# A Fourier filter and a gated feed-forward block in one kernel: the first transform step on sums and differences of rows, in 32x32 tiles

## Chip, cores, metric

The kernel runs on one core of one Trainium2 chip. The metric is the device time of one launch in microseconds (us). Its engines are named as in the profile: PE (TensorE, matmuls; PEld its weight loads), DVE (VectorE), ACT (ScalarE), POOL (GpSimd) and SP (SyncE, which only issues DMAs). ACT and POOL issue DMAs too.

## The reference

```python
batch, seq, dim = (8, 3008, 256)              # d_ff = 1536

def _attn_ref(x, filt_r, filt_i):
    X = np.fft.rfft(x, axis=1)
    F = (filt_r + 1j * filt_i)[None, :, :]
    return np.fft.irfft(X * F, n=x.shape[1], axis=1)

def _moe_ref(x, w_gate, w_val, w_out):        # x: (8 * 3008, 256)
    g = x @ w_gate
    silu = g * (1.0 / (1.0 + np.exp(-g)))
    return silu * (x @ w_val) @ w_out
```

All is float32. The first function filters each of the 8 batches along its 3008 tokens; the second is applied to every token of the result.

## The kernel before

**Two kinds of work in one stream.** The feed-forward block of batch b and the Fourier filter of batch b + 1 run side by side. A batch has 12 steps (`Group`: four chunks of tokens by three groups of hidden columns). Each step follows one written order of 174 tokens, `SCHEDULE`: a token names one small piece of work, and every engine gets its instructions in the order of the tokens (`pin` keeps the program's order). The tokens that the text needs:

- `Q0`, `P1`, `Q2` ...: matmuls of two 188-column halves into a PSUM bank k0 to k3 (L1075, tiles wk); `A13`, `A01`, `B..`, `E..` likewise into banks a.. and e.. (wa, we). `W1`, `W2`, `W6`: matmuls of the output projection (L1172, tiles wA, wF, wG).
- `f1`: ACT writes k1 negated into SBUF (L1090). `c1`, `c0`: ACT copies k1 and k0 (L1094). `g1`, `g0`: ACT's silu (L1117).
- `x03`, `s13`, `s01`: DVE combines a bank k with f1 or with a difference D (`D01`, by POOL); `s13` and `s01` write it into the banks a13 and a01 (L1097), to which `A13` and `A01` then add. `y01`: DVE combines k1 with c0 (L335). `h0`, `h1`: DVE's product with g0, g1 (L1122).
- `o1`, `o2`: the projection's sums, by DVE or, for the first of three groups, ACT (L328, L1184). `z0.o`: a DVE transpose, after the third group only. `x0.o` and so on: output stores.
- `b0` to `b7`: one part each of a burst of the next batch's filter. They stand at places 5, 10, 11, 33, 37, 95, 104 and 117 of the 174.

The order around the change, in one step:

```
Q0 o3' z1.o' t4.2' W2 b0 f0 S00' S01' i0 b1 b2 x0.o' t0.0 x1.o' i1 Q1 t0.1 x2.o' P3 x3.o' f1 t4.3'
W1 x4.o' S10' x03 S11' D01 i2 i3 i4 s13 b3 x5.o' P1 o1 b4 t0.2 P0 o2 z0.o c1 i5 A13 g1 c0 S20' Q2
S21' g0 y01 m13 t1.0 h0 f2 s01 W6 t1.1 h1 x23 D02 P2 o6 D12 A01 ...
```

PSUM has seven banks in turn for these tiles (pool `wps`, `NB`). After use of a part of `wt_t`, SP loads the next step's weights into it (`reload_weights`, L493), and waits for the matmuls that still read it.

**The filter's bursts.** From batch 2 on, the transform goes in two kinds of bursts, run during the batch before: `quads(g)`, g = 0 to 3, in steps 0 to 3, and `fours(w)`, w = 0 to 6, in steps 4 to 10. `load` is a DMA on SP (L618).

`quads` does the transform over 47 rows. A piece u holds four columns of rows n and the same four 32 further; rows lie on partitions 0 to 46 and 64 to 110. At `b0` there are eight matmuls (L716, tiles wqa, 47 rows in, 64 columns out, 512 elements). At `b1` and `b2` ACT copies one bank of a piece and DVE forms the difference and the sum with the other bank. At `b3` and `b4` ACT issues the stores of the two pieces to DRAM (`d1`, L733) and SP the loads of the next ones (`load_x`). `load_x(0)` and `load_x(1)` come in step 11 of the batch before.

`fours` loads these rows again (`load_four`), does a second transform step, and multiplies with the filter. For the complex product it swaps rows of a copy by DMA (`lent<-raw`), and multiplies by an imaginary part of the filter whose sign alternates by row. The rows with the other sign were negated once: during batch 1, `negated_filter` loads them to SBUF, ACT negates them (L323), and they are stored to `f_dram`; `keep_filter` copies the others in DRAM.

**Places in memory.** `room_of(tag)` gives parts of one SBUF tile, `lent`: `x` (two rooms), `y`, `g`, `e`, `t`, `tb`, `f`. `quads` uses x, y and g; `fours` uses the others too.

Of the kernel before, what the change touches and what calls it, by code (L numbers as in the profile page):

```python
# [41 lines left out]
FP32 = mybir.dt.float32  # L42
# [57 lines left out]
S00 S01 W1 S20 S21 S10 S11 W5 o1 W2 o5 S30 S31 W6 o2 z0.o o6 W3 o3 z1.o x0.o x1.o x2.o x3.o x4.o  # L100
x5.o W7 q4 o7 z3.o W4 o4 z2.o X0.o X1.o X2.o X3.o X4.o X5.o
""".split()
FILTER_AT = ("f1", "P0", "Q2", "h0", "g3", "A12", "Q0", "P1", "c1", "h1")
BLOCKS = (0, 1, 3, 2)
PAIRS = ((0, 1), (1, 2), (2, 3), (0, 2), (1, 3), (0, 3))
PAIRS_USED = ((1, 3), (0, 1), (0, 2), (1, 2), (2, 3), (0, 3))
# [19 lines left out]
def dft_tables():  # L126
# [40 lines left out]
    quad = np.zeros((128, 64))  # L167
    for h, turn in enumerate((ph, ph + 2 * np.pi * s / (2 * N1))):
        cols = np.stack([np.cos(turn), -np.sin(turn)], 2).reshape(N1, 2 * NS)
        quad[64 * h:64 * h + N1, 0:2 * NS] = cols  # L170

    four = np.zeros((128, N_FOUR + 1, 2, 4, 64))
    lo, qq = np.arange(32), np.arange(32)
# [32 lines left out]
def kernel(  # L206
# [60 lines left out]
    def weights_of(b, k, g):  # L267
        return wt_1 if b == 0 and k < NT and g == 1 else wt_t

    dram_tiles = [wdpool.tile([2 * NS, N2, C], FP32, name=f"d{1 + i % 2}_{i // 2}")  # L270
                  for i in range(4)]
    yt_dram = [wdpool.tile([128, 3 * len(PAIRS), TQ], FP32, name=f"yt_{k}") for k in range(NT)]
    y_dram = [wdpool.tile([128, 8, TQ], FP32, name=f"y_{k}") for k in range(NCHUNK)]
    o_dram = [wdpool.tile([128, 4 * NH, RP], FP32, name=f"o_{k}") for k in range(NT)]
# [32 lines left out]

    def keep_filter(n):

        part, r, e, half = (0, 0, 1)[n // 4], (0, 1, 1)[n // 4], n // 2 % 2, n % 2  # L310
# [4 lines left out]
    def negated_filter(w, stage):  # L315

        t = room_of("et"[w % 2])[0:64].rearrange("p (s c) -> p s c", c=C)
        if stage == 0:
            for q in range(4):
                pin(nc.sync.dma_start(out=t[16 * q:16 * q + 16],  # L320
                                      in_=filter_rows(1, q // 2, q % 2, 4 * w, 4)))
        elif stage == 1:
            pin(nc.scalar.mul(t, t, -1.0))  # L323
        else:
            pin(nc.sync.dma_start(out=f_pairs[:, 0, 1, 4 * w:4 * w + 4], in_=t))

    def add(eng, dst, a, b):
        return eng.tensor_tensor(out=dst, in0=a, in1=b, op=ALU.add)  # L328
# [246 lines left out]
    def load_back():  # L575

        t = rpool.tile([128, 2, 128], U32, name="quad", tag="pw", bufs=3)
        t = t.bitcast(FP32).rearrange("p b f -> p (b f)")
        quad_t.append(t)
        pin(nc.sync.dma_start(out=t[:, 0:64], in_=quad_dram.ap()))  # L580
# [19 lines left out]
    class Spectral:  # L600


        def __init__(self, b):
            self.b = b
            self.d1, self.d2 = [dram_tiles[2 * (b % 2) + i] for i in range(2)]
# [93 lines left out]
        def bank(self, name):  # L699
# [2 lines left out]
                return bank(name).rearrange("p (i c) -> p i c", i=NV)  # L702
            return fbank(name)

        def quads(self, g):

            pieces = (2 * g, 2 * g + 1)
            banks = {}
            for u in pieces:
                xt = self.x.pop(u)  # L710
                for h in range(2):
                    banks[u, h] = bank(f"qa_{self.b}_{u}_{h}")
                for cp in range(2):
                    for h in range(2):
                        r = slice(64 * h, 64 * h + N1)
                        pin(nc.tensor.matmul(  # L716
                            out=banks[u, h][64 * cp:64 * cp + 64], lhsT=quad_t[0][r, 0:64],
                            rhs=xt[r, 2 * cp:2 * cp + 2].rearrange("p n c -> p (n c)"),
                            start=True, stop=True))
            yield  # L720
            t1 = {u: room_of("yg"[i]).rearrange("p (n h c) -> p n h c", h=2, c=C)
                  for i, u in enumerate(pieces)}
            for u in pieces:
                low, high = [banks[u, h].rearrange("p (n c) -> p n c", c=C) for h in range(2)]
                pin(nc.scalar.copy(out=t1[u][:, :, 0], in_=low))
                pin(sub(nc.vector, t1[u][:, :, 1], t1[u][:, :, 0], high))
                pin(add(nc.vector, t1[u][:, :, 0], t1[u][:, :, 0], high))
                yield
            d1 = self.d1.rearrange("a (n h) c -> a n h c", h=2)
            for u in pieces:  # L730
                for cp in range(2):
                    n = 4 * u + 2 * cp
                    pin(nc.scalar.dma_start(out=d1[:, n:n + 2], in_=t1[u][64 * cp:64 * cp + 2 * NS]))  # L733
                self.load_x(u + 2)
                yield
            if g == 3:
                self.load_filter(0)
                self.load_turns(0)
            yield
            if g == 3:  # L740
                self.load_four(0)

        def load_four(self, w):

            if w < N_FOUR:
                t = self.t2[w] = room_of("t").rearrange("p (s h c) -> p s h c", h=2, c=C)
                d1 = self.d1.rearrange("(s r) (n h) c -> s (r n) (h c)", r=2, h=2)
                for p in range(2):
                    s = 4 * w + 2 * p
                    self.load(out=t[64 * p:64 * p + 64].rearrange("p s h c -> p s (h c)"),  # L750
                              in_=d1[s:s + 2].rearrange("s q c -> q s c"))

        def load_filter(self, w):

# [10 lines left out]
        def fours(self, w):  # L765
# [615 lines left out]
    for b in range(B):  # L1381
# [36 lines left out]
        for step in range(NCHUNK * NG + (b == B - 1)):  # L1418
# [16 lines left out]
            for place, token in enumerate(SCHEDULE):  # L1435
# [31 lines left out]
                    continue  # L1467
                if b == 0 and (step, op) == (5, "A23"):
                    nxt.load_two(0)
                if b + 2 < B and (step, op) in ((11, "Q2"), (11, "B01")):  # L1470
                    following.load_x(int(op == "B01"))
                if b == 1 and step < 4 and op in FILTER_AT:
                    n = FILTER_AT.index(op)
                    if n < 4 and step < 3:
                        keep_filter(4 * step + n)
                    elif 4 <= n < 6 and step < 3:
                        negated_filter(2 * step + n % 2, 0)
                    elif n >= 6 and step:
                        negated_filter(2 * step - 2 + n % 2, n // 2 - 2)
# [43 lines left out]
```

## Time and profile before

| | |
|---|---|
| median of 3 runs | 2825.41 us (2821.07 to 2829.73) |
| profiled execution | 2823.7 us; its span in the trace 2821.6 us; granted PE clock 0.997 |
| busy | PE 2787.5, PEld 2319.9, DVE 1999.1, ACT 1564.7, POOL 1579.9 us |
| DMA | 586.59 MB, mean 208 GB/s; the SP queue's packets took 60.8% of 16 engines' span, ACT's 5.7% |
| `quads` matmuls, L716 | 384 records of 589 ns (median), two for each of 192 instructions |
| `quads` copies and sums | ACT 48 of 586 ns; DVE 48 of 684 and 48 of 687 ns |
| `quads` stores, L733 | 96 issues on ACT, 308 to 2747 ns, median 435 |
| negation, L323 | 6 on ACT, 1057 ns each |

A group line of the profile reads: line, engine, operation, what is written and read with shapes, count, busy time and mean, then the idle time of that engine before it with what ended it. A timeline line reads: start in us from the span's start, length, engine, line, operation, tiles and shapes, count, and in brackets the idle time before it with what ended it. `ACTq` and `SPq` are the instruction queues of ACT and SP, which issue DMAs. Times of single steps count from the span's start.

### The profile page before, as it was taken

The page shows a single profiled execution, that of the slowest core. Times are in us where ns is not written, and L with a number is a line of the kernel's source. Part 1 is how long each engine was busy: PE and PEld are TensorE (multiplying, and loading weights), DVE is VectorE, ACT ScalarE, POOL GpSimd, SP SyncE. Part 2 cuts the span into 40 slices and gives each one's busy share as a digit, 9 for nine tenths or more (in the row PEclk, how much of TensorE's full clock was granted, in tenths as well). Part 3 has the DMA queues.
Part 4 walks back from the last instruction along what each step waited for, and adds up shares of the span by engine and source line. Part 5 has one row for each costly group of instructions (what it writes and reads, how often), then busy time and mean ns, then how long its engine had stood idle before and what let it go on. Part 6 is the DMA issues. An engine that isn't in the chain of part 4 may idle for free.

```text
span 2821.6 us, 48540 instructions
## 1 busy us (share of the span) xinstructions
PE 2787.5 (99%) x15444; PEld 2319.9 (82%) x15444; DVE 1999.1 (71%) x4579; ACT 1564.7 (55%) x4176; POOL 1579.9 (56%) x1689
## 2 busy tenths in 40 slices
PE   8999999999999999999999999999999999999998
PEld 6877888888888888788888888878888888888887
DVE  7898767767667766667766677667676767666666
ACT  5675455555555555555555555555555555555554
POOL 4786576465545565456653566445655455545544
PEclk9999999999999999999999999999999999999999
DMA  9687876877666775667666676667766677654443
GB/s 214 224 272 237 283 242 211 285 233 232 181 188 207 246 221 175 204 215 229 222 185 197 211 246 201 188 190 236 228 205 181 213 224 227 192 153 148 153 137 82
DMA packets 362933, 586.59 MB, mean 208 GB/s; under 512 B 198620, under 2 KB 245660, under 8 KB 362536
## 3 DMA queue, kind: packets, MB, share of 16 engines
q1 hardware_dynamic: 337722, 533.61, 60.8%
q10 hardware_dynamic: 22318, 44.38, 5.7%
q0 software_dynamic: 2640, 5.51, 0.7%
q8 instruction: 125, 2.05, 0.3%
q14 instruction: 128, 1.05, 0.1%
HBM read 467.48 MB, written 101.34 MB: 202 GB/s over the span
## 4 chain that ended last, share of the span: by engine, by line
PE 91%; POOL 2%; DVE 2%; DMA 1%; issue 1%; ACT 1%; ACTq 0%; SPq 0%; POOLq 0%; DVEq 0%
PE wa L1075 25%; PE wk L1075 17%; PE wA L1172 16%; PE we L1075 13%; PE wG L1172 8%; PE wF L1172 4%; PE pd L978 3%; PE wqa L716 2%; PE wqc L775 1%; PE wqb L787 1%; POOL out_dram L1157 0%; POOL h L331 0%; PE pa L857 0%; DMA lent<-later_tbl 0%; PE pd L981 0%
## 5 line engine op out<-in xcount | busy, mean ns | idle before, releaser
L1075 PE MATMUL wa<-y_t,wt_t 128*128 128x188 f32 x4464 | 881.6, 324 | 4.0 <-DVE wa L1097 2.3
L1075 PEld LDWEIGHTS wa<-y_t,wt_t 128*128 128x128 f32 x4464 | 749.8, 191 | 79.5 <-ACT wa L1101 9.3
L1075 PEld LDWEIGHTS wk<-y,wt_t 128*128 128x128 f32 x2976 | 495.0, 190 | 109.5 <-issue 33.4
L1075 PE MATMUL wk<-y,wt_t 128*128 128x188 f32 x2976 | 572.0, 325 | 3.2 <-ACT f L1090 3.2
L331 POOL TENSOR_TENSOR h<-h 128x376 f32<-128x376 f32 x572 | 559.6, 1000 | 15.4 <-DVE h L328 15.2
L328 POOL TENSOR_TENSOR h<-h 128x376 f32<-128x376 f32 x190 | 182.8, 983 | 685.5 <-DVE h L1122 685.5
L1172 PE MATMUL wA<-h,wo_t 128*128 128x376 f32 x1532 | 551.8, 482 | 3.9 <-DVE o L328 2.1
L1075 PE MATMUL we<-y_t,wt_t 128*128 128x188 f32 x2232 | 431.7, 323 | 1.6 <-ACT we L1106 1.5
L331 POOL TENSOR_TENSOR D<-f,f 128x376 f32<-128x376 f32 x288 | 280.0, 986 | 258.4 <-ACT f L1090 256.0
L331 DVE TENSOR_TENSOR we<-we,m 128x376 f32<-128x376 f32 x576 | 319.8, 556 | 141.1 <-PE we L1075 73.9
L1075 PEld LDWEIGHTS we<-y_t,wt_t 128*128 128x128 f32 x2232 | 369.3, 190 | 2.7 <-ACT we L1106 2.1
L1172 PEld LDWEIGHTS wA<-h,wo_t 128*128 128x128 f32 x1532 | 274.9, 190 | 113.7 <-issue 7.0
L1110 ACT COPY m<-wa 128x376 f32<-128x376 f32 x576 | 272.7, 473 | 102.0 <-PE wa L1075 98.8
L335 DVE SCALAR_TENSOR_TENSOR y<-wk,c 128x376 f32<-128x376 f32 x480 | 244.8, 541 | 63.8 <-ACT c L1094 37.8
L1117 ACT ACTIVATE g<-wa 128x188 f32<-128x188 f32 x576 | 187.5, 326 | 164.7 <-PE wa L1075 154.9
L1117 ACT ACTIVATE u<-we 128x188 f32<-128x188 f32 x576 | 188.7, 328 | 160.2 <-DVE we L331 153.3
L1172 PE MATMUL wG<-h,wo_t 128*128 128x376 f32 x768 | 274.0, 479 | 0.0
L1094 ACT COPY c<-wk 128x376 f32<-128x376 f32 x288 | 136.5, 474 | 226.0 <-PE wk L1075 196.7
L1090 ACT ACTIVATE f<-wk 128x376 f32<-128x376 f32 x288 | 140.4, 488 | 168.6 <-PE wk L1075 118.0
L1106 ACT COPY we<-y 128x376 f32<-128x376 f32 x480 | 222.3, 480 | 19.8 <-DVE h L1122 14.4
L1122 DVE TENSOR_TENSOR h<-wa,g 128x188 f32<-128x188 f32 x576 | 199.4, 347 | 38.0 <-ACT g L1117 37.6
L1122 DVE TENSOR_TENSOR h<-we,u 128x188 f32<-128x188 f32 x576 | 198.5, 345 | 28.8 <-ACT u L1117 17.3
(193 smaller groups left out, 3523.0 us busy)
## 6 DMA issues: line engine op xcount, KB each, us to landing
wt_t<-w_all SPq DMA_DIRECT2D x174, 896.0 KB
wt_t<-w_all SPq DMA_DIRECT2D x174, 768.0 KB
lent<-filter SPq DMA_DIRECT2D x36, 1024.0 KB
lent<-d SPq DMA_DIRECT2D x84, 256.0 KB
d<-lent ACTq DMA_DIRECT2D x84, 256.0 KB
d<-lent ACTq DMA_DIRECT2D x96, 192.0 KB
lent<-raw SPq DMA_DIRECT2D x144, 128.0 KB
t<-d SPq DMA_DIRECT2D x114, 128.0 KB
```

What stands on the lines that cost most here:

```text
L328: return eng.tensor_tensor(out=dst, in0=a, in1=b, op=ALU.add)
L331: return eng.tensor_tensor(out=dst, in0=a, in1=b, op=ALU.subtract)
L335: return nc.vector.scalar_tensor_tensor(out=dst, in0=a, scalar=-1.0, in1=b, op0=ALU.mult, op1=ALU.subtract)
L978: pin(nc.tensor.matmul(out=rows, lhsT=self.t4[k, i][:, j, ts(cb, 128)], rhs=cols, start=j == 0, stop=True, skip_group_check=True))
L1075: pin(nc.tensor.matmul(out=ps[:, z], lhsT=self.wt[:, SLOT[p], z], rhs=rhs, start=start and z == 0, stop=True, skip_group_check=True))
L1090: pin(act.mul(self.small(f"f{i}", f"f{i}", 1), t[f"k{i}"], -1.0))
L1094: pin(act.copy(out=self.small(f"c{i}", f"c{i}", 1), in_=t[f"k{i}"]))
L1106: pin(act.copy(out=self.bank(f"e{at}"), in_=t[f"y{at}"]))
L1110: pin(act.copy(out=self.small(f"m{at}", "m", 4), in_=t[f"a{at}"]))
L1117: pin(act.activation(out=self.small(op, "g", 3, 1)[:, 0], in_=ps[:, 1], func=AF.Silu))
L1122: pin(v.tensor_tensor(out=dst, in0=ps[:, 0], in1=g, op=ALU.mult))
L1172: pin(nc.tensor.matmul(out=self.tiles[at], lhsT=wo_t[:, JB * q + i, WO[p], :], rhs=self.hs[i][:, HID[p]], start=start and i == 0, stop=Tru ...
```

## The change

From batch 2 on, `quads` works on sums and differences of rows. Row n and row 47 - n of the transform have the same cosine and opposite sines; so 24 sums and 24 differences take the place of 47 rows. The falling rows must first lie in rising order: `turn_rows` copies them in DRAM, row by row, into `turned_dram`. `load_x(g)` loads 32 rising rows for 16 columns (four DMAs, 128 partitions in all) and the turned rows in one DMA of 512 KB. `fold(g)` makes the sums in room `e` and the differences in room `t`, four DVE instructions of 128x512. Those of group g + 1 stand at `b4` to `b7` of the burst before; those of group 0 in step 11 (`first_fold`).

A burst has 16 matmuls of 24 rows in and 32 columns out. The order of what follows changes as well: at `b1` the copy and both sums of the first piece, at `b2` the copy of the second piece and the stores of the first, at `b3` the sums of the second, at `b4` its stores. The rows go to `quads_dram` in a new order, 64 partitions a store for 48; `load_four` reads them with four DMAs for two.

The sign of the swapped rows is now put on by ACT as it copies them (`mul` with a column of +1 and -1 for `copy`). `negated_filter` is gone, and `keep_filter` copies all 16 parts.

```diff
-FILTER_AT = ("f1", "P0", "Q2", "h0", "g3", "A12", "Q0", "P1", "c1", "h1")
+FILTER_AT = ("f1", "P0", "Q2", "h0")
...
-                if u < N_QUAD:
-                    self.x[u] = room_of("x", u).rearrange("p (n c) -> p n c", c=C)
+                if u < N_QUAD // 2:
+                    self.x[u] = [room_of("x", n) for n in range(2)]
+                    up, down = self.x[u]
+                    at = self.turned.rearrange("(g q) p c -> g p q c", q=4)[u]
+                    self.load(out=down.rearrange("p (q c) -> p q c", c=C), in_=at)
                     rows = x[self.b].rearrange("(r n) c -> r n c", n=N2)
-                    for h in range(2):
-                        for a, e in ((0, 32), (32, N1)):
-                            self.load(out=self.x[u][64 * h + a:64 * h + e],
-                                      in_=rows[a:e, 32 * h + 4 * u:32 * h + 4 * u + 4])
+                    for n in range(4):
+                        first = 16 * n + 4 * u
+                        self.load(out=up[ts(n, 32)].rearrange("p (q c) -> p q c", c=C),
+                                  in_=rows[0:32, first:first + 4])
...
+        def turn_rows(self, *parts):
+            xb, to = x[self.b], self.turned
+            end = NS if self.b > 3 else 32
+            for part in parts:
+                h, lane, n = part // 2, 32 * part, 16 * part
+                p = 1 - h
+                self.load(out=to[:, lane + p:lane + end],
+                          in_=bass.AP(tensor=xb.tensor, ap=[[C, 16], [-N2 * C, end - p], [1, C]],
+                                      offset=xb.offset + ((N1 - 1) * N2 + n) * C))
+                if h == 0:
+                    self.load(out=to[:, lane], in_=xb[n:n + 16])
+
+        def fold(self, g):
+            if g < N_QUAD // 2:
+                up, down = self.x.pop(g)
+                self.x[g] = [room_of("e"), room_of("t")]
+                for t, f in zip(self.x[g], (add, sub)):
+                    for half in range(2):
+                        a = ts(half, NV * C)
+                        pin(f(nc.vector, t[:, a], up[:, a], down[:, a]))
+                        if t is self.x[g][1] and half:
+                            self.load_x(g + 1)
+                        yield
+
+        def first_fold(self):
+            for _ in range(4):
+                yield
+            yield from self.fold(0)
...
         def quads(self, g):
...
+            for cp in range(2):
+                for t in range(2):
+                    for i, u in enumerate(pieces):
+                        for h in range(2):
+                            r, c = 32 * (2 * h + i), 32 * (2 * cp + t)
+                            pin(nc.tensor.matmul(
+                                out=banks[u, h][c:c + 32], lhsT=quad_t[0][r:r + NS, ts(t, 32)],
+                                rhs=parts[t][r:r + NS, ts(cp, NV * C)],
+                                start=True, stop=True))
             yield
...
+            low(pieces[0])
+            both(pieces[0])
+            yield
+            low(pieces[1])
+            store(pieces[0])
+            yield
+            both(pieces[1])
+            yield
+            store(pieces[1])
+            next(fold, None)
+            yield
...
-                pin(nc.scalar.copy(out=t, in_=there[p]))
+                pin(nc.scalar.mul(t, there[p], quad_t[0][:, 64:65]))
...
+    for part, at in enumerate(((3, "E23"), (4, "A13"), (4, "E23"), (5, "A13"))):
+        chore(*at, lambda part: following.turn_rows(part), part)
...
+        if b + 2 < B:
+            bursts[-1] = following.first_fold()
...
-                if b + 2 < B and (step, op) in ((11, "Q2"), (11, "B01")):
-                    following.load_x(int(op == "B01"))
+                if b and b + 2 < B and (step, op) == (8, "Q0"):
+                    following.turn_rows(0, 1, 2, 3)
+                if b + 2 < B and (step, op) == (11, "Q0"):
+                    following.load_x(0)
```

`low(u)` is the ACT copy of a piece's first bank, `both(u)` the two DVE instructions, `store(u)` the two store DMAs on ACT. The table for the matmuls is rewritten to 24 rows of cosines and of sines, and gets the column of signs.

More of the change, by code (lines that the diff above doesn't have):

```diff
@@ L165, in dft_tables @@
                 back[row:row + rows, first + N1 * i:first + N1 * (i + 1)] = one_hi[a:a + rows]
[L167 to L170, printed above, removed]
+    quad = np.zeros((4, 32, 2, 32))
+    for h in range(2):
+        turn = 2 * np.pi * (np.outer(2 * n1[0:NS] + h, s) % (2 * N1)) / (2 * N1)
+        quad[2 * h:2 * h + 2, 0:NS, 0, 0:NS], quad[2 * h:2 * h + 2, 0:NS, 1, 0:NS] = np.cos(turn), -np.sin(turn)
+        quad[2 * h:2 * h + 2, 23 * h] *= np.array([0.5, 0.0])[:, None]
+    quad = np.concatenate([quad.reshape(128, 64), np.tile([[1.0], [-1.0]], (64, 1))], 1)
     four = np.zeros((128, N_FOUR + 1, 2, 4, 64))
@@ L271 @@
                   for i in range(4)]
+    quads_dram = [wdpool.tile([64, N2, C], FP32, name=f"quads_{i}") for i in range(2)]
+    turned_dram = [wdpool.tile([16, 128, C], FP32, name=f"turned_{i}") for i in range(2)]
     yt_dram = [wdpool.tile([128, 3 * len(PAIRS), TQ], FP32, name=f"yt_{k}") for k in range(NT)]
@@ L308, in keep_filter @@
     def keep_filter(n):
-        part, r, e, half = (0, 0, 1)[n // 4], (0, 1, 1)[n // 4], n // 2 % 2, n % 2
+        part, r, e, half = n // 8, n // 4 % 2, n // 2 % 2, n % 2
         q = 32 * e + 16 * half
@@ L313, in keep_filter @@
                               in_=filter_rows(part, e, half, 0, NS)))
[L315 to L325, printed above, removed]
     def add(eng, dst, a, b):
@@ L579, in load_back @@
         quad_t.append(t)
-        pin(nc.sync.dma_start(out=t[:, 0:64], in_=quad_dram.ap()))
+        pin(nc.sync.dma_start(out=t[:, 0:65], in_=quad_dram.ap()))
         t = rpool.tile([128, 2, 128, 2], U32, name="back", tag="raw", bufs=2)
@@ L604, in __init__ @@
             self.b = b
+            self.quads_dram, self.turned = quads_dram[b % 2], turned_dram[b % 2]
             self.d1, self.d2 = [dram_tiles[2 * (b % 2) + i] for i in range(2)]
@@ L703, in bank @@
             return fbank(name)
-        def quads(self, g):
[L707 to L719, printed above, removed]
+        def turn_rows(self, *parts):
[9 more added lines that the diff above has]
+                    self.load(out=to[:, lane], in_=xb[n:n + 16])
@@ new lines, in first_fold @@
+        def first_fold(self):
+            for _ in range(4):
+                yield
+            yield from self.fold(0)
+        def quads(self, g):
+            pieces = (g, g + N_QUAD // 2)
+            banks = {(u, h): bank(f"qa_{self.b}_{u}_{h}") for u in pieces for h in range(2)}
+            parts = self.x.pop(g)
+            for cp in range(2):
+                for t in range(2):
+                    for i, u in enumerate(pieces):
+                        for h in range(2):
+                            r, c = 32 * (2 * h + i), 32 * (2 * cp + t)
[3 more added lines that the diff above has]
+                                start=True, stop=True))
@@ L720, in quads @@
             yield
+            fold = self.fold(g + 1)
             t1 = {u: room_of("yg"[i]).rearrange("p (n h c) -> p n h c", h=2, c=C)
                   for i, u in enumerate(pieces)}
[L723 to L728, printed above, removed]
@@ L729, in quads, with low, both @@
-            d1 = self.d1.rearrange("a (n h) c -> a n h c", h=2)
-            for u in pieces:
+            views = {key: t.rearrange("p (n c) -> p n c", c=C) for key, t in banks.items()}
+            def low(u):
+                pin(nc.scalar.copy(out=t1[u][:, :, 0], in_=views[u, 0]))
+            def both(u):
+                pin(sub(nc.vector, t1[u][:, :, 1], t1[u][:, :, 0], views[u, 1]))
+                pin(add(nc.vector, t1[u][:, :, 0], t1[u][:, :, 0], views[u, 1]))
+            d1 = self.quads_dram.rearrange("a (n h) c -> a n (h c)", h=2)
@@ L731, in quads, with store @@
+            def store(u):
                 for cp in range(2):
                     n = 4 * u + 2 * cp
-                    pin(nc.scalar.dma_start(out=d1[:, n:n + 2], in_=t1[u][64 * cp:64 * cp + 2 * NS]))
-                self.load_x(u + 2)
-                yield
+                    pin(nc.scalar.dma_start(out=d1[:, n:n + 2], in_=t1[u][64 * cp:64 * cp + 64]))
+            low(pieces[0])
[4 more added lines that the diff above has]
+            yield
@@ L738, in quads @@
                 self.load_turns(0)
+            next(fold, None)
             yield
@@ L741, in quads @@
                 self.load_four(0)
+            next(fold, None)
+            yield
+            next(fold, None)
         def load_four(self, w):
@@ L746, in load_four @@
                 t = self.t2[w] = room_of("t").rearrange("p (s h c) -> p s h c", h=2, c=C)
-                d1 = self.d1.rearrange("(s r) (n h) c -> s (r n) (h c)", r=2, h=2)
+                d1 = self.quads_dram.rearrange("(r s) (n h) c -> r n s (h c)", r=2, h=2)
                 for p in range(2):
                     s = 4 * w + 2 * p
-                    self.load(out=t[64 * p:64 * p + 64].rearrange("p s h c -> p s (h c)"),
-                              in_=d1[s:s + 2].rearrange("s q c -> q s c"))
+                    for r in range(2):
+                        a = 64 * p + 32 * r
+                        self.load(out=t[a:a + 32].rearrange("p s h c -> p s (h c)"),
+                                  in_=d1[r, :, s:s + 2])
         def load_filter(self, w):
@@ L1469 @@
                     nxt.load_two(0)
-                if b + 2 < B and (step, op) in ((11, "Q2"), (11, "B01")):
-                    following.load_x(int(op == "B01"))
+                if b and b + 2 < B and (step, op) == (8, "Q0"):
+                    following.turn_rows(0, 1, 2, 3)
+                if b + 2 < B and (step, op) == (11, "Q0"):
+                    following.load_x(0)
                 if b == 1 and step < 4 and op in FILTER_AT:
                     n = FILTER_AT.index(op)
[L1474 to L1479, printed above, removed]
+                    keep_filter(4 * step + n)
                 if b and chunk and op == "B01":
```

## The prediction

> **What bounds the kernel now.** I read the page's busy table and chain first, then what the changed step costs (the timeline of the weight loads around its first burst), then the timelines of TensorE, ScalarE and VectorE over the start of one step that holds such a burst.
>
> ```profile
> PE 2787.5 (99%) x15444; PEld 2319.9 (82%) x15444; DVE 1999.1 (71%) x4579; ACT 1564.7 (55%) x4176; POOL 1579.9 (56%) x1689
> ...
> PE 91%; POOL 2%; DVE 2%; DMA 1%; issue 1%; ACT 1%; ACTq 0%; SPq 0%; POOLq 0%; DVEq 0%
> ```
>
> TensorE is busy 99% of the span and is 91% of the chain, so a microsecond taken from it counts if nothing else arrives late. How little may arrive late is seen only inside a step.
>
> ```profile
> 449.56 0.21 PEld L716 LDWEIGHTS wqa<-lent,quad 47*64 47x64 f32 x8 [0.53 <-issue]
> 450.05 0.15 PEld L716 LDWEIGHTS wqa<-lent,quad 47*64 47x64 f32 x4 [0.28 <-issue]
> 450.48 0.15 PEld L716 LDWEIGHTS wqa<-lent,quad 47*64 47x64 f32 x4 [0.28 <-issue]
> ```
>
> The eight matmuls of a burst (16 records, two passes each) run as four waves of four 64x64 tiles, some 0.43 us apart.
>
> ```profile
> 1529.50 1.95 PE L716 MATMUL wqa<-lent,quad 47*64 47x512 f32 x16
> 1531.38 1.54 PE L1075 MATMUL wk<-y,wt_t 128*128 128x188 f32 x8
> ...
> 1535.42 0.80 PE L1075 MATMUL wa<-y_t,wt_t 128*128 128x188 f32 x4
> ...
> 1538.60 1.44 PE L1075 MATMUL wa<-y_t,wt_t 128*128 128x188 f32 x8
> ```
>
> ```profile
> 1530.64 0.59 ACT L725 COPY lent<-wqa 128x512 f32<-128x512 f32 x1 [1.75 <-PE wqa L716]
> 1531.49 0.59 ACT L725 COPY lent<-wqa 128x512 f32<-128x512 f32 x1 [0.27 <-PE wqa L716]
> 1532.38 0.48 ACT L1090 ACTIVATE f<-wk 128x376 f32<-128x376 f32 x1 [0.29 <-PE wk L1075]
> 1532.70 2.29 ACTq L733 DMA_DIRECT2D d<-lent  x4
> 1535.03 0.47 ACT L1094 COPY c<-wk 128x376 f32<-128x376 f32 x1 [2.16 <-DMA d<-lent]
> ```
>
> ```profile
> 1533.30 0.69 DVE L328 TENSOR_TENSOR lent<-lent,wqa 128x512 f32<-128x512 f32 x1
> 1533.90 0.54 DVE L1097 SCALAR_TENSOR_TENSOR x<-wk,f 128x376 f32<-128x376 f32 x1
> 1534.36 0.55 DVE L1097 SCALAR_TENSOR_TENSOR wa<-wk,f 128x376 f32<-128x376 f32 x1
> 1534.82 0.54 DVE L328 TENSOR_TENSOR o<-o,wA 128x376 f32<-128x376 f32 x1
> ...
> 1536.13 0.55 DVE L335 SCALAR_TENSOR_TENSOR y<-wk,c 128x376 f32<-128x376 f32 x1 [0.19 <-ACT c L1094]
> 1536.60 0.34 DVE L1122 TENSOR_TENSOR h<-wk,g 128x188 f32<-128x188 f32 x1
> 1536.86 0.55 DVE L1097 SCALAR_TENSOR_TENSOR wa<-wk,D 128x376 f32<-128x376 f32 x1
> ```
>
> The burst takes 1.88 us, to the wk matmuls. The wa at 1535.42 is A13 and adds to what VectorE's s13 (1534.36) wrote: 0.51 us of slack. The wa at 1538.60 is A01, on s01 (1536.86 to 1537.41): 1.19 us. ScalarE's c copies come straight after the four store issues: its queue stood in them (2.16 <-DMA d<-lent).
>
> **What the Trainium skill says.** "TensorE: Matmul & The Clock Gate", Measured speedup vs the span model: sixteen 32x32 tiles (K=M=32, N=512) gave 10.6 times one tile's rate, so sixteen at once is possible; this trace shows four at once only. "Perfetto Trace Analysis", DMA Instruction — HWDGE: the issuing sequencer itself waits for the semaphores and is held until the descriptors are made. The trace agrees (the 2.16 us). "VectorE: DVE Perf Modes", Why `tensor_tensor` can't do 2×_2P or 4×: both read ports are taken, so sums from SBUF are no faster; the trace agrees, 683 ns at L845 (SBUF) and 684 with PSUM (L331).
>
> **The change, part by part.**
>
> *Matmuls.* Per burst 16 instructions on 16 tiles, 32 records in two waves for four. Two waves of 0.43 go, 12 more starts of 7 ns in a wave come: 0.86 - 0.08 = 0.78 us less. 24 bursts (4 in each of 6 batches): 18.7 us, all on TensorE's path. From below: no saving, if only some tiles run at once.
>
> *Evacuation, order on ScalarE.* Before, both copies stood ahead of f1 and all stores behind it. Now low(p0), low(p1) and the two stores of p0 stand before f1, and the stores of p1 before c1. A store waits for VectorE's two sums, and behind it on ScalarE stand f1 (VectorE's s13 and GpSimd's D01 wait for it) and then c1, g1, c0 (y01, h0 and s01 wait for these). In the step above, with its durations: low(p0) 1530.7 to 1531.3 (two waves earlier than the last copy, but the whole burst must be through); sums 0.69 + 0.03 + 0.69, to 1532.75; two issues (0.31 and 0.44 with 0.04 around each) to 1533.55; f1 to 1534.1; s13 to 1534.65; A13, ready at 1534.64, loses 0.05. Sums of p1 to 1536.0; two issues to 1536.8; c1 1536.85, c0 0.59 later, ending 1537.9; y01 1537.95; s01 starts 0.73 after it (as now) and ends 1539.23; A01 starts at 1539.27, not 1538.60: **+0.67** where the matmuls alone would give -0.78. W6 waits for o1 (before, 1.34 us of slack) on the same chain and adds nothing beyond. VectorE alone: 1536.0 + o1 0.55 + new sum 0.68 + o2 0.55 = 1537.8, just below c0's time.
>
> The four steps differ. In a batch's step 0 a transpose (0.58) stands before y01: about 1538.35, so +1.07. In step 1 stage-3 matmuls (0.8) lie before A01, which starts 11.89 us into the step now and 11.77 then: -0.12. Steps 2 and 3: +0.67 each (step 3 has no new sum, but c0 decides). Per batch 1.07 - 0.12 + 0.67 + 0.67 = 2.3; six batches **+13.8 us**. The stores carry 64 rows for 48 (256 KB for 192); issues were 0.31 to 2.75 us, median 0.435. I take 0.1 us more a burst: +2.4. From below 0; from above 0.5 a burst, +12.
>
> *Second sums.* 16 VectorE adds a batch (96, 683 ns each, 65.6 us) at b4 to b7. The first is in the chain above. The others lie where VectorE has gaps of 0.7 to 0.9 us, and the `fours` of steps 5 and 8 already put two such VectorE products at b5 and b6 without TensorE waiting: 0. If that cover is gone, at most 0.68 for each of 72: I keep +10 as the bound.
>
> *First fold, last step of a batch.* Its load starts where it starts now (SP issued it 0.37 us behind the last weight reload):
>
> ```profile
> 758.95 0.32 SPq L493 DMA_DIRECT2D wt_t<-w_all  x1
> 759.32 1.79 SPq L618 DMA_DIRECT2D lent<-in_x_dram  x4
> ```
>
> The 376 KB landed by 765.45 by the semaphores. Now 1 MB: 512 packets of 1 KB (46 ns each on 16 engines, 1.5 us) and a third more of 4 KB (0.4): 767.3. VectorE gets there at 766.0, stalls 1.3, adds 0.68; s01 then ends at 769.95 (gaps take back 0.5), and A01 starts at 770.51. Cover 0.55 us: I take 0.2 a batch, +1. If it lands 2 us later, +1.5 a batch, +9.
>
> *Row copies.* Six DMAs a batch on SP ahead of the waiting reload in step 8 (about 3 us of issue, before a wait that SP has anyway from 677.5 to 682.8), 2016 packets of 1 KB: 5.9 us of all engines (b over 3: 4.4). Swapped rows queue behind them: landing about 13 us into the step, not 10.7; VectorE uses them at 14 to 15. ScalarE's two stores there may be issued slower: +1, from 0 to +5. In batch 0 the copies go beside weight preparation: +0.5, 0 to +3.
>
> *Negated filter.* 30 SP DMAs, six ScalarE products (1.06 us), gone; 4 copies of 384 KB come. Batch 1's step 3 loses 1.4 us now behind a ScalarE queue held by stores (one issue 2.75 us), part of which may go: -1.
>
> *Signs, loads.* 72 copies become products with a column: some 14 ns each (L1090's 488 against L1094's 474) on ScalarE, 1 us in gaps: 0. 12 more load_four issues and 12 fewer x issues a batch: SP waits for TensorE most of its time: 0.
>
> Sum: 13.8 + 2.4 + 1 + 1 + 0.5 - 1 = about **+17 us**. Against the profiled execution (2823.7, span 2821.6): 2841; against the median of the runs, 1.7 higher, **2842**.
>
> **Rivals.**
> (a) *Faster*: the shorter burst is kept, 18.7 less small losses: 2808. Against it: A01 has 1.19 us of slack, and the gain itself takes 0.78 of it; it needs f1 and c0 not to be held by the stores. Decides if s01 ends by 1537.8. Chance 0.12.
> (b) *No change*: the stores hold f1 and c0 only in part. With VectorE alone deciding, s01 comes at about 1538.2 in step 2, so each burst keeps 0.3: -7; with half of the chain, 0: 2818 to 2834. Chance 0.18.
> (c) *The chain as worked out*: 2834 to 2860, chance 0.57.
> (d) *Worse*: the first fold's load is late, or the later sums reach TensorE: 17 + 9 to 10 and more, 2850 to 2865; chance 0.08.
> (e) *Sixteen tiles don't run at once*: four at a time makes eight waves, six more than in (c), so the copies start 2.6 us later, 24 x 2.6 = 62 more: 2904. Chance 0.05.
>
> **How the numbers follow.** A measurement here can tell 0.3%, 8.5 us, from no change. Faster 0.12 (a), same 0.18 (b), slower 0.70 (c, d, e). The time is (c)'s. The range 2815 to 2862 leaves out most of (a), (e) and the end of (d), under 0.2 together; (c) alone is 2834 to 2860.
>
> **What would show it.** Right: the burst about 1.1 us long with 32 records; f1 idle before it with the store's issue (DMA or VectorE) named; c behind a second store; A01's idle of about 1.4 us with VectorE wa as releaser, in steps 0, 2 and 3 of batches 1 to 6; steps (first wk matmul to first wk matmul in the timeline) of 29.2, 29.2, 27.6, 27.6 us becoming about 30.3, 29.1, 28.3, 28.3. Wrong: no TensorE idle before A01, or the copies starting over 2 us after the burst began.

## Result, and the profile after

| | before | after |
|---|---|---|
| median | 2823.65 us (2821.07 to 2829.73) | 2872.01 us (2870.88 to 2875.55) |
| ratio | | 1.017 (95% interval 1.015 to 1.019) |
| profiled execution, span | 2823.7, 2821.6 us | 2871.0, 2869.2 us |
| ACT's `quads` stores, median | 0.435 us | 0.556 us |

The change makes the kernel slower by 48 us. The prediction was 2842 us, with a range up to 2862: the direction was right, the size was not. All lines of this section are of the changed kernel. Busy times and the chain of waits come first:

```profile
PE 2788.5 (97%) x15828; PEld 2308.9 (80%) x15828; DVE 2059.9 (72%) x4675; ACT 1555.5 (54%) x4170; POOL 1582.9 (55%) x1689
...
PE 76%; DVE 3%; ACT 2%; DMA 2%; ACTq 1%; issue 1%; SPq 0%; POOL 0%; POOLq 0%; DVEq 0%
```

TensorE is busy for as long as before (2788.5 and 2787.5 us) in a span that is 48 us longer, and its part of the chain falls from 91% to 76%. So the loss is time in which TensorE waits. The list of waits, TensorE alone, names them (what waited, what for, us in total, times, longest):

```profile
PE wk L1123 <- ACT f L1138: 46.1, 49, 1.8
PE wa L1123 <- DVE wa L1145: 8.3, 4, 4.2
```

The same entry of the kernel before is `PE wk L1075 <- ACT f L1090: 3.2, 3, 1.6`. Of the 49 waits for ScalarE's `f`, 48 lie in the 24 bursts' steps, two in each. The start of a step (batch 4's step 2; in the step shown before, the burst starts at 1529.50, here at 1558.45) shows where. First TensorE:

```profile
1558.45 1.14 PE L743 MATMUL wqa<-lent,quad 24*32 24x512 f32 x32
1559.53 1.75 PE L1123 MATMUL wk<-y,wt_t 128*128 128x188 f32 x8
1561.11 1.43 PE L1220 MATMUL wA<-h,wo_t 128*128 128x376 f32 x4
1563.54 1.54 PE L1123 MATMUL wk<-y,wt_t 128*128 128x188 f32 x8 [1.00 <-ACT f L1138]
1564.92 0.80 PE L1123 MATMUL wa<-y_t,wt_t 128*128 128x188 f32 x4
1565.55 0.85 PE L1123 MATMUL wk<-y,wt_t 128*128 128x188 f32 x4
1566.24 1.43 PE L1220 MATMUL wA<-h,wo_t 128*128 128x376 f32 x4
1568.67 0.90 PE L1123 MATMUL wk<-y,wt_t 128*128 128x188 f32 x4 [1.00 <-ACT f L1138]
1569.41 0.80 PE L1123 MATMUL wa<-y_t,wt_t 128*128 128x188 f32 x4
```

The burst works: the next matmul comes 1.08 us after its start, and came 1.88 after it. The first wait is at P1 (with P0, the eight `wk` at 1563.54), the second at P2 (1568.67), each 1.00 us. A13 (1564.92) and A01 (1569.41), which the prediction watched, start straight behind them and wait for nothing. ScalarE in the same stretch:

```profile
1559.73 1.07 ACT L754 COPY lent<-wqa 128x512 f32<-128x512 f32 x2 [1.89 <-PE wqa L743]
1561.79 1.11 ACTq L765 DMA_DIRECT2D quads<-lent  x2
1563.00 0.48 ACT L1138 ACTIVATE f<-wk 128x376 f32<-128x376 f32 x1 [2.20 <-PE wA L1220]
1565.41 1.11 ACTq L765 DMA_DIRECT2D quads<-lent  x2
1566.56 0.47 ACT L1142 COPY c<-wk 128x376 f32<-128x376 f32 x1 [3.08 <-PE wk L1123]
1566.93 0.33 ACT L1165 ACTIVATE g<-wk 128x188 f32<-128x188 f32 x1
1567.15 0.48 ACT L1142 COPY c<-wk 128x376 f32<-128x376 f32 x1
1567.50 0.36 ACT L1165 ACTIVATE g<-wk 128x188 f32<-128x188 f32 x1
1567.72 0.50 ACT L1158 COPY m<-wa 128x376 f32<-128x376 f32 x1
1568.08 0.54 ACT L1138 ACTIVATE f<-wk 128x376 f32<-128x376 f32 x1
```

ScalarE's second copy ends at 1560.80, and then it stands for a microsecond, until VectorE has made both sums of the first piece (done at 1561.76), to issue two stores. Only then comes f1 (its bracket names PE, but the line above it, the queue's two issues from 1561.79 to 1562.90, is what it stands behind). It reads bank k1 between Q1, which wrote it, and P1, which adds to it: P1 starts 0.06 us after f1's end. Then it stands again for the sums of the second piece, and behind these stores are c1, g1, c0, g0, m13 and f2, back to back. f2 reads bank k2 between Q2 and P2: P2 starts 0.05 us after f2's end. VectorE in the same stretch (lines left out are its other work):

```profile
1561.07 0.69 DVE L320 TENSOR_TENSOR lent<-lent,wqa 128x512 f32<-128x512 f32 x1
1561.68 0.54 DVE L1145 SCALAR_TENSOR_TENSOR x<-wk,f 128x376 f32<-128x376 f32 x1
1563.52 0.56 DVE L1145 SCALAR_TENSOR_TENSOR wa<-wk,f 128x376 f32<-128x376 f32 x1 [1.30 <-ACT f L1138]
...
1564.70 0.69 DVE L320 TENSOR_TENSOR lent<-lent,wqa 128x512 f32<-128x512 f32 x1
1565.30 0.54 DVE L320 TENSOR_TENSOR o<-o,wA 128x376 f32<-128x376 f32 x1
1565.76 1.22 DVE L320 TENSOR_TENSOR lent<-lent 128x512 f32<-128x512 f32 x1
```

VectorE loses 1.30 us to f1, and so the second piece's sums, the stores that wait for them and f2 come late as well. VectorE itself holds no matmul here: s13 ends at 1564.08 and s01 at 1568.94, before A13 (1564.92) and A01 (1569.41) have their turn.

The Trainium skill ("PSUM — Partial Sum Buffer", PSUM bank collisions raise a hardware error) says that a bank must be guarded by semaphores when one engine writes it and another reads it. The trace agrees that the program does so: matmuls that add to a bank stand until the engine that reads it between them is done, here 1.00 us of idle time each.

Step durations (first `wk` matmul to first `wk` matmul, us) and the batch:

| | step 0 | 1 | 2 | 3 | batch |
|---|---|---|---|---|---|
| before, batch 4 | 29.21 | 29.21 | 27.61 | 27.61 | 339.9 |
| after, batch 4 | 31.32 | 30.28 | 29.78 | 29.59 | 347.3 |
| before, batch 1 | 29.21 | 29.07 | 27.47 | 29.00 | 341.1 |
| after, batch 1 | 32.01 | 37.05 | 29.81 | 29.58 | 354.7 |

Batches 2 to 6 lose 7.3 to 7.6 us each (37.1 in all), batch 1 loses 13.7; batches 0 and 7 and the stretch ahead of them give back 3.2. That is the span's 47.6. In batch 4 the delays at P1 are 1.19, 1.19, 1.17 and 1.16 us and those at P2 1.17, 0.36, 1.17 and 1.17: 8.6 together. (Delays are counted, here and below, from the matmul's due start, 0.17 us before the idle time in brackets begins.) The four shorter bursts give 3.2 back; some 2 us lie in delays under 0.25 us.

Batch 1's step 1 holds one thing more. SP's queue there:

```profile
467.82 0.37 SPq L611 DMA_DIRECT2D lent<-turned  x1
485.20 1.80 SPq L611 DMA_DIRECT2D lent<-in_x_dram  x4
487.09 2.84 SPq L485 DMA_DIRECT2D wt_t<-w_all  x2
```

and VectorE's first of the second sums behind it:

```profile
491.79 0.69 DVE L320 TENSOR_TENSOR lent<-lent 128x512 f32<-128x512 f32 x1 [6.02 <-DMA lent<-in_x_dram]
```

Between the load of the turned rows and that of the rising rows, SP stands for 17 us. The next group's second sums wait for the late rows, s01 for them on VectorE, and A01 4.4 us for s01 (4.2 of them idle time, the longest of the waits for `wa` above). What SP waits for is the completion semaphore of that load, which DMAs of SP and ScalarE use in turn (in the trace, 105 for both). It stands there behind a store that ScalarE issues only in the step after: issued at 482.18, landed at 485.18, 0.02 us before SP goes on.

### The profile page after: what moved, and what is told of

It is laid out like the page before. It is cut to its first block, busy times and chain, and to the rows that moved or that the text cites. A ratio compares the mean times of both kernels' runs of the same rounds, so it can differ in the third digit from the quotient of the medians.

```text
span 2869.2 us, 49234 instructions
## 1 busy us (share of the span) xinstructions
PE 2788.5 (97%) x15828; PEld 2308.9 (80%) x15828; DVE 2059.9 (72%) x4675; ACT 1555.5 (54%) x4170; POOL 1582.9 (55%) x1689
## 4 chain that ended last, share of the span: by engine, by line
PE 76%; DVE 3%; ACT 2%; DMA 2%; ACTq 1%; issue 1%; SPq 0%; POOL 0%; POOLq 0%; DVEq 0%
PE wa L1123 22%; PE wA L1220 13%; PE wk L1123 13%; PE we L1123 11%; PE wG L1220 7%; PE wF L1220 4%; PE pd L1026 3%; DMA quads<-lent 2%; PE wqc L823 1%; PE wqb L835 1%; DVE lent L323 1%; PE wqa L743 1%; DVE lent L320 1%; ACT c L1142 1%; ACTq L765 1%; DVE o L320 1%
## 5 line engine op out<-in xcount | busy, mean ns | idle before, releaser
L1123 PE MATMUL wa<-y_t,wt_t 128*128 128x188 f32 x4464 | 881.9, 324 | 9.0 <-DVE wa L1145 7.4
L1123 PEld LDWEIGHTS wa<-y_t,wt_t 128*128 128x128 f32 x4464 | 749.4, 191 | 85.5 <-ACT wa L1149 9.5
L1123 PEld LDWEIGHTS wk<-y,wt_t 128*128 128x128 f32 x2976 | 489.3, 190 | 177.2 <-ACT f L1138 75.4
L1123 PE MATMUL wk<-y,wt_t 128*128 128x188 f32 x2976 | 583.0, 328 | 46.5 <-ACT f L1138 46.1
L1123 PE MATMUL we<-y_t,wt_t 128*128 128x188 f32 x2232 | 433.0, 323 | 2.0 <-ACT we L1154 1.5
L1123 PEld LDWEIGHTS we<-y_t,wt_t 128*128 128x128 f32 x2232 | 368.7, 190 | 6.2 <-DVE we L327 4.0
L1138 ACT ACTIVATE f<-wk 128x376 f32<-128x376 f32 x288 | 140.9, 490 | 214.6 <-PE wk L1123 126.0
L1170 DVE TENSOR_TENSOR h<-we,u 128x188 f32<-128x188 f32 x576 | 197.8, 344 | 29.0 <-ACT u L1165 17.5
```

Of the source, the lines that this page charges most:

```text
L1123: pin(nc.tensor.matmul(out=ps[:, z], lhsT=self.wt[:, SLOT[p], z], rhs=rhs, start=start and z == 0, stop=True, skip_group_check=True))
L1138: pin(act.mul(self.small(f"f{i}", f"f{i}", 1), t[f"k{i}"], -1.0))
L1170: pin(v.tensor_tensor(out=dst, in0=ps[:, 0], in1=g, op=ALU.mult))
```

## Experiments

**My theory** after reading this profile: ScalarE's queue, held by the stores, keeps f1 and f2 from the banks that P1 and P2 write. **Rivals**: the 96 added sums on VectorE; the larger stores or the new DRAM traffic; and, for batch 1, the filter copies. Ratios are to the kernel before on the same chip, 2821.0 us in the first four runs and 2822.4 in the last four.

**Both pairs of stores one place later** (`e1_stores_later`). From the changed kernel:

```diff
             low(pieces[1])
-            store(pieces[0])
             yield
             both(pieces[1])
+            store(pieces[0])
             yield
-            store(pieces[1])
             next(fold, None)
             yield
+            store(pieces[1])
```

> The changed kernel with the stores of the first piece moved from b2 to b3 (behind f1) and those of the second from b4 to b5 (behind c1, c0 and f2); the new sum of b4 stays. Theory, ScalarE's queue is held: TensorE's waits for f1 (1.16 us) and f2 (1.17) go, a burst keeps the 0.81 us that its matmuls save, less what VectorE's chain to s01 still costs in steps 0 and 2 (0.3 to 1.2): 2808 to 2822 us. Rival, VectorE's second sums are the cost: f1 and f2 are still late, 2860 or more. Rival, the larger DMA traffic: 2860 or more.

Measured: 2811.36 us, ratio 0.9963 (0.995 to 0.9976). The losses at P1 and P2 are gone, and batch 4 takes 338.9 us (29.24, 28.48, 27.68, 27.15 in steps 0 to 3). Its ScalarE, over the same part of a step:

```profile
1522.72 1.07 ACT L754 COPY lent<-wqa 128x512 f32<-128x512 f32 x2 [1.89 <-PE wqa L743]
1523.68 0.50 ACT L1138 ACTIVATE f<-wk 128x376 f32<-128x376 f32 x1
1524.78 1.10 ACTq L765 DMA_DIRECT2D quads<-lent  x2
1526.20 0.47 ACT L1142 COPY c<-wk 128x376 f32<-128x376 f32 x1 [2.02 <-PE wk L1123]
```

f1 follows the copies at once, and TensorE waits for none of the same stores behind it. The order of two tokens' work is worth 60 us.

**The new order alone, in the kernel before** (`e2_order_alone`): the old 47-row bursts with four waves and stores of 48 rows, no sums ahead, but `low`, `both` and `store` in the new order:

```diff
-            for u in pieces:
-                low, high = [banks[u, h].rearrange("p (n c) -> p n c", c=C) for h in range(2)]
-                pin(nc.scalar.copy(out=t1[u][:, :, 0], in_=low))
...
-                yield
...
+            low(pieces[0])
+            both(pieces[0])
+            yield
+            low(pieces[1])
+            store(pieces[0])
+            yield
+            both(pieces[1])
+            self.load_x(pieces[0] + 2)
+            yield
+            store(pieces[1])
+            self.load_x(pieces[1] + 2)
+            yield
```

> The kernel before (64x64 tiles, no sums of rows, no copies) with the changed kernel's order of evacuation alone: first copy and both its sums, second copy, stores of the first piece, sums of the second, stores of the second. Theory: f1 ends at 6.5 us into the step where P1 is ready at 6.64, so no wait there; f2 ends at 11.4 where P2 is ready at 10.46 (11.26 in step 1): 0.95 us in three steps and 0.15 in one of each batch, 18 us in all: 2836 to 2848 us. Both rivals: as before, 2825 us.

Measured: 2841.61 us, 1.0074 (1.0057 to 1.0091): the order by itself loses some 20 us. Its TensorE waits:

```profile
PE wk L1089 <- ACT f L1104: 15.4, 19, 1.7
PE wa L1089 <- DVE wa L1111: 3.6, 2, 2.7
```

Steps 0, 2 and 3 of six batches account for 18 of the 19, all at P2. There is none at a burst's P1, but only just: in batch 4's step 2, f1 ends 4.57 us after the burst's start and P1 is due at 4.65. In the changed kernel's step above these are 5.03 and 3.92. P1 comes 0.73 us sooner there because the burst is shorter; f1 comes 0.46 us later, for the most part because the first pair of stores takes 1.11 us to issue and not 0.79. So the shorter burst does more than the longer issues to bring P1 into the wait: part of its gain turns into waiting.

**Only the first piece's stores later** (`e3_first_store`):

```diff
             low(pieces[1])
-            store(pieces[0])
             yield
             both(pieces[1])
+            store(pieces[0])
             yield
             store(pieces[1])
```

> The changed kernel with only the first piece's stores moved, from b2 to b3 behind f1. Theory: the wait for f1 goes, sums and stores of the second piece come 1.3 us sooner, f2 ends about 10.8 us into the step where P2 is ready at 9.9: a wait of 0.9, about what the matmuls save. 2822 to 2834 us. Rivals: 2860 or more.

Measured: 2845.79 us, 1.0087 (1.0072 to 1.0102), above what I expected. The part that this was to show came out: no wait at P1, f2 still late at P2 by 1.1 us, batches 2 to 6 at 341.7 us. The miss lies in batch 1, 354.5 us: SP's stand is there as well (its loads of rising rows begin at 467.02 and go on after 486), and A01 waits 4.0 us in step 1 and 3.5 us in step 2.

**All four stores issued by SP, at the places of the change** (`e4_stores_sp`):

```diff
-    pin(nc.scalar.dma_start(out=d1[:, n:n + 2], in_=t1[u][64 * cp:64 * cp + 64]))
+    pin(nc.sync.dma_start(out=d1[:, n:n + 2], in_=t1[u][64 * cp:64 * cp + 64]))
```

> The changed kernel with the four stores of a burst at their places in the order, but issued by SP in place of ScalarE: same bytes, same VectorE work. Theory: f1 and c1 are free as with the later stores, 2805 to 2825 us, with SP waiting for VectorE where it has time. Rival, VectorE's sums or the traffic: 2860 or more.

Measured: 2811.19 us, 0.9964 (0.9951 to 0.9977), the same as with the stores moved. The bytes, their destination and VectorE's sums are those of the changed kernel; only the queue that stands for the sums is another. That rules out the bytes of the larger stores and the DRAM traffic. How long the issues take still counts where ScalarE makes them.

**The second sums on 16 columns for 512** (`e5_small_sums`):

```diff
                         a = ts(half, NV * C)
+                        a = slice(half * NV * C, half * NV * C + 16)
```

> The changed kernel, with each second-sum instruction cut from 512 columns to 16; the other columns of the rooms e and t keep old values, so the sums are mostly left out. Theory (ScalarE's queue, held by the stores, keeps f1 and f2 from the banks that P1 and P2 write): the waits for f1 and f2 stay and the time stays near the changed kernel's, 2860 to 2870 us. Rival (the 96 added VectorE sums are the loss): 80 of them lie within the steps, at some 0.6 us each; if they are on the path, the time falls to 2825 to 2835 us.

Measured: 2869.7 us, 1.0165 (1.0152 to 1.0179): as slow as the changed kernel. The groups of these instructions on VectorE, first of the changed kernel, then of this one (count, busy us, mean ns, idle before):

```profile
L320 DVE TENSOR_TENSOR lent<-lent 128x512 f32<-128x512 f32 x48 | 44.5, 928 | 17.9 <-DMA lent<-in_x_dram 17.9
L323 DVE TENSOR_TENSOR lent<-lent 128x512 f32<-128x512 f32 x48 | 34.5, 718 | 0.0
```

```profile
L320 DVE TENSOR_TENSOR lent<-lent 128x16 f32<-128x16 f32 x48 | 19.6, 408 | 17.2 <-DMA lent<-in_x_dram 17.2
L323 DVE TENSOR_TENSOR lent<-lent 128x16 f32<-128x16 f32 x48 | 12.5, 261 | 0.0
```

VectorE loses 47 us of work (79.0 against 32.1), and TensorE still waits 43.8 us for `f`. `e1_stores_later` and `e4_stores_sp`, with the sums whole, are fast. The sums are not the cause.

**Batch 1's filter copies issued at the start of the step** (`e7_filter_at_start`):

```diff
-FILTER_AT = ("f1", "P0", "Q2", "h0")
+FILTER_AT = ("Q0", "Q1", "W1", "P1")
```

> The changed kernel; only the four filter copies in each of batch 1's first four steps are issued at the tokens Q0, Q1, W1, P1 and not f1, P0, Q2, h0. With this order the row loads of batch 1 stand behind no store of a later step on their completion semaphore. Theory (SP's 17 us stand in batch 1 is a wait for a store that ScalarE issues only in the next step, and costs 7 us): SP goes on within 1 us there, step 1 of batch 1 takes 30 to 31 us for 37.05, and the time is 2863 to 2867 us. Rival (the filter copies' traffic or the first use of the pattern in batch 1 is what makes that step long): step 1 of batch 1 stays near 37 us and the time near 2872 us.

Measured: 2864.05 us, 1.0148 (1.0134 to 1.0162), and step 1 of batch 1 takes 30.27 us for 37.05. SP's queue in the same place:

```profile
466.21 0.37 SPq L611 DMA_DIRECT2D lent<-turned  x1
466.63 1.89 SPq L611 DMA_DIRECT2D lent<-in_x_dram  x4
```

No load, store or sum is added or taken away; SP goes on at once. The copies' traffic is as before, so it was the wait, at about 7 us (354.7 less 347.7 for the batch).

**The same with the first piece's stores later** (`e8_first_store_filter`), both diffs above together:

> The changed kernel with the stores of the first piece at b3 and the filter copies of batch 1 at Q0, Q1, W1, P1: the kernel that took 2845.79 us, with only batch 1's wait of SP taken away. Theory: batch 1 falls from 354.5 to 342 us, the other batches stay at 341.7, the time is 2830 to 2836 us, and each burst still waits for f2 at P2. Rival (the excess over 2829 was not that wait): 2842 to 2848 us.

Measured: 2832.52 us, 1.0035 (1.0022 to 1.0049). So some 13 us of the version of 2845.79 were SP's stand. What is left over the version with both stores moved, 21 us, is about P2's wait for f2: `PE wk L1123 <- ACT f L1138: 20.7, 20, 2.0` in its list of waits. And what it gains on `e7_filter_at_start`, 31.5 us, is the first pair of stores. Batch 1 took 345.3 us, not 342: one store issue of 1.57 us in its step 0 made P2 wait 2.05 us.

**All together, with the second sums later** (`e6_best`): stores as in `e1_stores_later`, filter copies as above, and the sums at b5, b6 and two new places, b8 and b9, where VectorE has gaps. From `e1_stores_later`, without the line of the filter copies and one that counts the two new tokens:

```diff
-l02 B12 v12 E13 t3.1 h02 u02 A23 n2 l13 g12 v02 W5 s03 e23 h12 e01 m23 A03 o5 z3.o u13 E23 t3.2 m03
+l02 B12 v12 E13 t3.1 h02 u02 A23 n2 l13 g12 v02 W5 s03 e23 h12 b8 e01 m23 A03 o5 z3.o b9 u13 E23 t3.2 m03
...
-            for _ in range(4):
+            fold = self.fold(0)
+            for n in range(10):
+                if n in (5, 6, 8, 9):
+                    next(fold, None)
                 yield
-            yield from self.fold(0)
...
-            next(fold, None)
             yield
...
             next(fold, None)
+            yield
+            yield
+            next(fold, None)
             yield
```

> The changed kernel with the stores at b3 and b5, as in the version of 2811 us, and also the second sums at b5, b6 and two new places b8 (after h12) and b9 (after o5) in place of b4 to b7, and the filter copies at Q0, Q1, W1, P1. Theory: A01's wait of 0.52 us in step 0 and the waits of 0.2 to 0.7 us at E in steps 0 and 2 came from the sums at b4 and b7, and go: 2804 to 2809 us. Rival (the late sums delay the combinations that follow them, E23 and E01, as much): 2810 to 2818 us.

Measured: 2805.32 us, 0.9936 (0.9922 to 0.995): faster than both kernels, 17.1 us below the one before. Of the 24 bursts' 0.81 us each, 19.4 in all, most is kept (where P1 is due, 0.73 of each is left, 17.5 in all). In batch 2 steps 0 and 2 take 28.71 and 26.87 us, for 29.24 and 27.22 in `e1_stores_later`, and the waits of A01 in step 0 and of the E matmuls are gone: with the stores out of the way, it was the sums at b4 and b7 that held them.

## Why the prediction was right or wrong

**Matmuls: right.** 0.78 us less a burst was predicted, 0.81 measured (1.88 to 1.08, with rounding). Sixteen tiles run at once: in the step shown the 32 matmuls start in two groups of 16, 0.45 us apart. Rival (e) falls. The first matmuls behind the burst follow each other more slowly than before, so that 0.73 is left where P1 is due; the prediction had no such term.

**Evacuation, order on ScalarE: this step failed.** That the stores would hold f1 and c, and so turn the gain into a loss, was right, and so were the times up to there: sums of the first piece done 3.25 us after the burst's start by the prediction (1532.75), 3.31 in the trace. The step then followed f1 only to its readers, s13 with A13 and s01 with A01. It left out that f1 and f2 also free something: banks k1 and k2, which P1 and P2 add to. P1 stands ahead of A13. By the prediction's own times (f1 done at 1534.1; P1, at 1534.15 before, due 0.78 sooner) P1 would have lost 0.8 us where it has "A13 loses 0.05"; it lost 1.17. P2 stands ahead of A01 in the same way. So TensorE's waits lie at P1 and P2, and A01 has none in the steps where the prediction expected one, which it had named as a sign of being wrong. The group of these matmuls in the page of before gave the hint, in its last columns:

```profile
L1075 PE MATMUL wk<-y,wt_t 128*128 128x188 f32 x2976 | 572.0, 325 | 3.2 <-ACT f L1090 3.2
```

All of TensorE's waiting ahead of `wk` was for `f`: the dependence was there, and only its slack was large. By P1 and P2 the loss per batch is 8.6 less 3.2 for the bursts, and with the small delays the batch loses 7.3; the prediction's net was 2.3.

How much of the size each part explains can be estimated by redoing the prediction's chain with figures of the trace (times from the burst's start; the prediction has A01 at 9.77 us). With store issues of 1.06 us a pair and not 0.75, A01 comes at 10.39. With P2 on f2 as what A01 stands behind, and not s01, it comes at 10.82. The trace has 10.96. So of the 1.2 us that the chain missed, about half lie in the length of the store issues, and a third in the bank that f2 frees.

**The four steps.** 30.3, 29.1, 28.3 and 28.3 us were predicted, 31.3, 30.3, 29.8 and 29.6 came. Step 1 differs from the others as predicted, but at P2 (0.36 us), where its stage-3 matmuls cover f2. The prediction's terms add to 17.7 us, not 17. Its terms for the bursts, 13.8 and 2.4, stand against 50.8 us that the six batches lost, 7 of them by SP's stand in batch 1.

**Larger stores: this term was mis-sized.** 0.31 + 0.44 us for a pair became 0.45 + 0.61 with 64 rows: 0.3 us a pair, two pairs a burst, where 0.1 a burst was taken. As they lie ahead of f1 and f2, that counts in full in the working above.

**"W6 adds nothing beyond", second sums 0: right for the wrong reason.** TensorE's waits for `o` at the projection are 2.1 us in all before and after. The second sums held hardly any matmul in the changed kernel (cut to 16 columns, they leave batch 4 at 346.7 us for 347.3), because ScalarE, behind the stores, was later still. The exception is batch 1, where they were themselves late. With the stores moved they count: A01 then waits 0.52 us in step 0, and moving the sums gains 6 us (2811.4 to 2805.3, with all else that `e6_best` changes), within the bound of 10.

**First fold, row copies, signs: right, all small.** Step 11 took 28.60 us in most batches, as before, and 30.20 once (batch 0) in the profiled execution, when the rows landed late; in the other kernels' executions that step of batch 0 took 28.60 to 29.10. Step 8, with the row copies, is 27.61 in batches 1 to 6 before and after.

**Negated filter: -1 predicted, some +6 measured** (batch 1 loses 13.7 us, the others 7.4 in the mean). Step 3 of batch 1 did lose its long store issue (29.00 us before, 27.61 in batch 4), but the new filter copies fell where SP's loads came to wait for a store of the step after, which costs 7 us (`e7_filter_at_start`). No step of the prediction asked which DMAs share a completion semaphore.

**Rivals.** Against (a) stood that the gain needs f1 and c0 not to be held; with that removed, (a)'s 2808 is about what came (2811, 2805). Rival (d) had the right side and the wrong mechanism.

## What to carry to other kernels

For every instruction that a change delays, ask two things: who reads what it writes, and who may overwrite what it reads. An evacuation that sits in the middle of an accumulation holds TensorE directly, with no VectorE in between. And a DMA issue that waits for another engine belongs behind everything on its queue that someone is waiting for, or on a queue with nothing urgent: the same stores made this change cost 48 us or gain 10.

## What the runs showed of the hardware beyond that

**A wait can cost twice.** Over the first 2.05 us of A01's idle time in batch 1 the granted clock is 1.00, over the rest 0.51, and over the next 4.6 us, when matmuls run again, 0.50. Eight `wa` took 2.87 us, as against 1.44 in the step shown of before:

```profile
494.17 2.87 PE L1123 MATMUL wa<-y_t,wt_t 128*128 128x188 f32 x8 [4.22 <-DVE wa L1145]
```

By an estimate from these figures, 4.6 us at half the clock cost 2.3 us more than at the full one. With A01's delay of 4.4 us that is 6.7 of the 7 us that SP's stand costs.

The Trainium skill ("TensorE: Matmul & The Clock Gate", What's actually happening) gives half rate after an idle window of about 3.4 us. Here less was enough twice: the 2.05 us above, and 1.89 us of idle time in `e8_first_store_filter`, where the granted clock is 0.50 from 458.2 to 461.3, after the matmuls had begun again at 456.61. The length of the idle time is not all that decides: 2.36 us of it in `e4_stores_sp`, up to 335.24, left the granted clock at 1.00 until 343, and so did the waits for `f` in the changed kernel, up to 1.8 us, in the 4 us after the longest. What else decides is not shown here.

**Sums from SBUF beside GpSimd.** The added sums took 0.68 us where nothing ran on GpSimd as they started (65 of 96), and 1.22 in the median in the 31 cases where something did. In the lines of the result, the sum at 1565.76 took 1.22 us; the same place in `e1_stores_later`, after GpSimd's end, took 0.68. Cut to 16 columns it still took 0.70 there: it ended at 1567.22, and GpSimd's products at 1567.19. The Trainium skill ("SBUF — State Buffer", SBUF: two separate sides) says that a VectorE operation with two SBUF inputs and GpSimd take turns at a shared pair of ports, each for a whole instruction; these numbers agree.
